# A new computed order of instructions for the first 28 slices of an attention and gated MLP kernel

## The chip, the cores and the metric

The kernel runs on one core of a Trainium2 chip. The metric is device time in microseconds (us) of one execution, taken as the median of several executions. The engines are TensorE (PE in the profile; its weight loads are PEld), VectorE (DVE), ScalarE (ACT), GpSimd (POOL) and SyncE (SP). One execution of each kernel was recorded by the hardware profiler; times inside a trace count from its first instruction. A run is called fast when it is within 1.5% of the fastest of its kernel; all comparisons below use fast runs.

## The reference, cut to what matters

```python
x: [8, 8, 512, 64]   state: [8, 8, 32, 64]
scores = x @ state^T / 8 ; a = softmax(scores)      # per batch and head
xread = a @ state                                   # 512 rows
sread = softmax(state @ x^T / 8) @ x                # 32 rows
rows = concat(xread, sread), heads side by side     # 8 * 544 rows of 512
out = (relu(rows @ w_gate) * (rows @ w_val)) @ w_out   # d_ff 1536
```

The kernel never forms xread. For each batch b it multiplies the state by the two weight matrices first (U = state @ w, in "c" and "u" units), and each of 12 slices of 128 hidden columns is then the product of U with the transposed softmax (the "gv" products). Relu on ScalarE and a multiplication on DVE turn a slice into columns of h, and "o" pieces multiply h by w_out.

## The kernel before

All parts are short functions, and a text called `program` lists the calls for the first 28 slices (all 12 of batches 0 and 1, four of batch 2). Each word is a call, and the digits behind `@` are the banks of PSUM (where this kernel's TensorE results go) that it takes. A product that takes a bank again waits for the bank's last reader: in the changed kernel's trace one began at 43.05 us, behind 0.39 us of idle time, just after that reader had ended at 42.99. A filler is a product that nobody reads; it is there only to keep TensorE busy. The instructions of an engine are issued in the order of the words, and where I compared the trace before with the words, the rows stand in that order: TensorE from 10.24 to 15.12 us. After the program a regular loop does the rest, unchanged.

```python
def u_unit(b, w, lo):                      # 512 columns of U: 8 products of 64 rows
    u_alloc(b)
    ps = held["u", b, w, lo] = [bank("up"), bank("up")]
    u_mm(ps, b, w, lo, 512)

def u_out(b, w, lo, kc, eng):              # their copy to SBUF, on act or dve
    copy[eng](out=U[b][:, w, kc, lo:lo + 512], in_=held["u", b, w, lo][kc])

def att_scale(b, jp, eng="dve"):           # word "nx": a_sn = e_sn / row sum
    ...tensor_tensor(out=by_pair(a_sn[b], jp)..., in0=e_v, in1=held["rc", b, jp]..., op=ALU.mult)

def x_next(b):                             # word "xn": casts of the next batch, then its transpose
    x_conv(b, 0, "pool")
    x_conv(b, 1, "pool")
    x_trans_dma(b)

# words: spin.n = n filler products; sc, ex, nr = scores, exponential, row sums; aT, ao = transpose
# of a_sn and its copy; re, mu = relu and multiplication of a slice; sr = state sums
for g in range(first, NF * (B + 1)):       # the loop; first = 28, so its first call is gv(2, 4)
    gv(b, jf) ... relu(b, jf) ; mult(b, jf) ; out_piece(...)
```

The softmax here doesn't subtract the row's maximum and nothing guards it: scores larger than these inputs give would overflow.

Of the kernel before, what the change touches and what calls it, by code (L numbers as in the profile page):

```python
# [16 lines left out]
def kernel(  # L17
# [52 lines left out]
    stT = const.tile([128, B, NJ, 64], BF16, name="stT")  # L70
# [5 lines left out]
    xf, xb, xT, e_sn, a_sn, ANS, U, hsb, sr_sb = {}, {}, {}, {}, {}, {}, {}, {}, {}  # L76
    copy = {"act": nc.scalar.copy, "dve": nc.vector.tensor_copy, "pool": nc.gpsimd.tensor_copy}

    given, turn = [], {"r": 0, "o": 0}

    def bank(name, kind="r"):

# [356 lines left out]
             "c": c_unit, "co": c_out, "u": u_unit, "uo": u_out, "gv": gv, "re": relu, "mu": mult, "o": out_part,  # L439
             "of": fin_x, "xn": x_next, "xp": x_pad, "sr": sr_mm, "sn": sr_norm}  # L440
    program = """
    dx.1.0.2 dx.1.1.2 stc.0.0.act stc.0.1.dve xc.0.0.act dw.0.0.128 spin.6 stT.0@5 xT.0.0@0 xc.0.1.dve dw.1.0.128 on
    sto.0.dve xT.0.1@4 xo.0.0.dve dw.0.128.128 xo.0.1.act dw.1.128.128 dw.0.256.256 spin.4 xT.0.3@2 dw.1.256.256
    xT.0.2@3 xo.0.3.dve sc.0.0@1 xo.0.2.act ex.0.0 sc.0.1@6 dw.0.512.256 xT2.1.0@5 ex.0.1 nr.0.0 xo2.1.0.act
    dw.1.512.256 spin.2 xT2.1.1@0 nr.0.1 xo2.1.1.act sc.1.0@4 dw.0.768.256 nx.0.0 dw.1.768.256 ex.1.0 spin.2
    c.1.0.128@23 nx.0.1 sc.1.1@1 co.1.0.128.1.act c.0.0.128@65 co.1.0.128.0.dve dw.0.1024.256 aT.0.1@0 ex.1.1
    co.0.0.128.0.dve aT.0.0@4 co.0.0.128.1.act ao.0.1.dve dw.1.1024.256 ao.0.0.act spin.1 c.1.128.128@32 nr.1.1
    c.0.128.128@16 co.1.128.128.1.act gv.0.0@50 co.0.128.128.0.act nr.1.0 co.0.128.128.1.act dw.0.1280.256 re.0.0
    gv.0.1@42 co.1.128.128.0.act nx.1.1 re.0.1 nx.1.0 dw.1.1280.256 c.0.256.256@17 c.1.256.256@65 co.0.256.256.1.act
    co.0.256.256.0.dve aT.1.0@3 aT.1.1@4 co.1.256.256.0.act ao.1.0.dve gv.0.2@71 dx.2.0.1 ao.1.1.dve  # L450
    co.1.256.256.1.act mu.0.1 re.0.2 gv.1.0@36 mu.0.0 ds re.1.0 mu.0.2 c.1.512.256@45 c.0.512.256@27
    co.1.512.256.0.act co.1.512.256.1.dve gv.1.1@03 co.0.512.256.1.act do.0.6 co.0.512.256.0.dve re.1.1 gv.1.4@14
    mu.1.0 xp.0 re.1.4 gv.1.3@57 mu.1.1 re.1.3 mu.1.4 gv.0.5@20 mu.1.3 do.6.12 re.0.5 gv.0.3@61 mu.0.5 xp.1 re.0.3
    c.0.768.256@35 c.0.1024.256@47 mu.0.3 co.0.768.256.1.act gv.1.2@20 co.0.1024.256.1.act co.0.768.256.0.dve df.3
    re.1.2 gv.0.4@61 co.0.1024.256.0.dve re.0.4 mu.1.2 gv.1.5@57 mu.0.4 re.1.5 gv.0.9@32 mu.1.5 re.0.9 gv.0.8@46
    mu.0.9 re.0.8 c.1.1280.256@01 c.0.1280.256@57 mu.0.8 co.1.1280.256.1.act xT2.2.1@3 co.0.1280.256.1.act
    co.1.1280.256.0.dve xT2.2.0@2 stc.1.0.pool co.0.1280.256.0.act c.1.768.256@46 xo2.2.1.dve stc.1.1.pool
    c.1.1024.256@17 xo2.2.0.act stc.3.0.pool gv.1.10@05 co.1.768.256.0.dve stc.2.0.pool co.1.768.256.1.dve
    co.1.1024.256.1.act stc.2.1.pool stT.1@3 gv.1.11@42 stc.3.1.pool re.1.10 sto.1.dve co.1.1024.256.0.act mu.1.10
    gv.0.11@76 re.1.11 re.0.11 mu.1.11 gv.1.7@30 mu.0.11 re.1.7 gv.1.9@15 mu.1.7 re.1.9 sc.2.0@4 gv.0.7@72 mu.1.9  # L460
    ex.2.0 re.0.7 nr.2.0 gv.0.6@36 re.0.6 mu.0.7 gv.0.10@01 mu.0.6 re.0.10 u.2.0.0@45 u.2.1.512@73 nx.2.0
    uo.2.0.0.1.act u.2.0.512@20 o.0.0@6 mu.0.10 uo.2.0.512.1.act uo.2.1.512.0.act uo.2.0.0.0.dve sc.2.1@5 o.0.1
    uo.2.0.512.0.act xn.3 uo.2.1.512.1.dve ex.2.1 u.2.1.1024@01 nr.2.1 u.2.1.0@42 uo.2.1.1024.0.act u.2.0.1024@35
    o.0.2 uo.2.1.0.1.act uo.2.0.1024.1.dve uo.2.1.0.0.act o.0.3@7 nx.2.1 of.0.0.dve aT.2.1@0 gv.1.8@25
    uo.2.1.1024.1.dve ao.2.1.act re.1.8 uo.2.0.1024.0.dve aT.2.0@4 o.0.4 ao.2.0.dve mu.1.8 gv.2.0@01 re.2.0 o.0.5
    mu.2.0 gv.2.2@23 of.0.1.act re.2.2 gv.1.6@45 mu.2.2 re.1.6 o.0.6@6 mu.1.6 o.0.7 o.0.8 gv.2.1@01 of.0.2.dve re.2.1
    gv.2.3@23 mu.2.1 re.2.3 o.0.9@7 mu.2.3 sr.0@4 sr.1@5 sn.0 sn.1 xp.2 xp.3
    """
    for word in program.split():
        word, _, banks = word.partition("@")  # L470
# [107 lines left out]
```

## Time and profile before

| | before |
|---|---|
| median | 224.28 us (224.14 to 224.79, 3 runs) |
| span in the trace | 222.9 us |
| first slice's product | 15.12 us |
| first product of the loop | 56.44 us |
| TensorE clock released to full speed | 10.21 us (fillers 0.427 us apart ahead of it, 0.22 after) |

The prediction below shows most of the lines. The columns are start, duration, engine, source line, operation, output and inputs, count and, in brackets, the idle time before it.

```profile
40.70 2.02 POOL L142 CAST xb<-xf 128x1024 bf16<-128x1024 f32 x2 [4.96 <-DMA xf<-in_x_dram]
```

The scaling is over before the two casts begin, at 1.0 us a cast. The 4.96 us of idle time ahead of the casts end when the transfer of x lands, so here the casts do not follow TensorE's pace.

### The profile page before, as it was taken

The numbers are of one execution on the slowest core, as the hardware profiler recorded it, in microseconds if no ns is written. First come the engines' busy times: TensorE is split into PE (matmuls) and PEld (weight loads), VectorE is DVE, ScalarE is ACT, GpSimd is POOL, SyncE is SP. The second block draws the span as 40 slices with busy tenths as digits, with TensorE's granted clock in tenths as the row PEclk, the third lists the DMA queues.
The fourth block names the chain that finished last, engine by engine and source line by source line (L and its number), as shares of the span: only waits on it lengthen the run. The fifth ranks groups of instructions, "written<-read, shape, count | busy, mean of one in ns | idle before, by whom it ended". The sixth has DMA issues, their size and how long they took to land.

```text
span 222.9 us, 4842 instructions
## 1 busy us (share of the span) xinstructions
PE 217.4 (98%) x1959; PEld 106.9 (48%) x1959; DVE 131.1 (59%) x233; ACT 123.2 (55%) x233; POOL 48.9 (22%) x54
## 2 busy tenths in 40 slices
PE   6999999999999999999999999999999999999994
PEld 2554454444544444444444444444444445666543
DVE  2399998965695559664877368646875433222100
ACT  4498788843567555574466456645654444222221
POOL 8877654300603334015000700000000000000000
PEclk9999999999999999999999999999999999999999
DMA  6999999152046771771169114511311111111132
GB/s 154 183 195 197 208 232 284 39 121 97 0 124 209 119 260 62 164 247 50 50 134 281 56 50 97 97 47 47 94 50 47 47 49 50 49 69 72 51 94 94
DMA packets 37799, 25.48 MB, mean 114 GB/s; under 512 B 18864, under 2 KB 33200, under 8 KB 37776
## 3 DMA queue, kind: packets, MB, share of 16 engines
q1 hardware_dynamic: 24912, 16.85, 26.3%
q0 software_dynamic: 11968, 7.47, 21.5%
q10 hardware_dynamic: 896, 0.85, 1.5%
q8 instruction: 15, 0.25, 0.4%
q14 instruction: 8, 0.07, 0.1%
HBM read 18.35 MB, written 8.91 MB: 122 GB/s over the span
## 4 chain that ended last, share of the span: by engine, by line
PE 95%; ACT 2%; DMA 1%; issue 0%; DVE 0%; DVEq 0%; ACTq 0%
PE o_ps L353 39%; PE gv_ps L316 38%; PE gv_ps L333 5%; PE up L291 4%; PE sc_ps L200 2%; DMA st_f<-in_state_dram 1%; PE sr_ps L264 1%; PE upc L291 1%; PE o_ps L379 1%; PE warm_ps L432 1%; PE xT_ps L186 1%; PE stT_ps L129 1%; PE xT_ps L169 1%; PE xT_ps L173 0%; ACT xT L189 0%; ACT e_sn L207 0%
## 5 line engine op out<-in xcount | busy, mean ns | idle before, releaser
L316 PE MATMUL gv_ps<-ans,U 128*128 128x512 bf16 x384 | 94.6, 379 | 0.3 <-ACT ans L249 0.3
L353 PE MATMUL o_ps<-wo_sb,h_sb 128*128 128x512 bf16 x372 | 94.8, 379 | 0.0
L340 ACT ACTIVATE g_sb<-gv_ps 128x512 bf16<-128x512 f32 (+1 forms) x108 | 62.5, 581 | 50.1 <-PE gv_ps L316 39.1
L344 DVE TENSOR_TENSOR h_sb<-gv_ps,g_sb 128x512 bf16<-128x512 f32 x96 | 64.7, 688 | 41.5 <-ACT g_sb L340 40.7
L316 PEld LDWEIGHTS <-U 128*128 128x128 bf16 x384 | 36.1, 98 | 40.7 <-issue 0.9
L353 PEld LDWEIGHTS <-h_sb 128*128 128x128 bf16 x372 | 35.3, 98 | 40.0 <-issue 1.6
L361 ACT COPY o_sb<-o_ps 128x512 f32<-128x512 f32 x29 | 17.1, 590 | 16.2 <-PE o_ps L353 16.2
L301 ACT CAST U<-up 128x512 bf16<-128x512 f32 x37 | 19.2, 594 | 11.1 <-PE up L291 11.1
L301 DVE CAST U<-up 128x512 bf16<-128x512 f32 x35 | 22.0, 682 | 2.3 <-PE up L291 1.9
L142 POOL CAST xb<-xf 128x1024 bf16<-128x1024 f32 x10 | 10.1, 1042 | 55.7 <-DMA xf<-in_x_dram 48.4
L256 POOL COPY xa<-xb 128x2048 bf16<-128x2048 bf16 (+1 forms) x9 | 15.6, 1748 | 13.9 <-issue 13.7
L213 DVE TENSOR_REDUCE cs<-e_sn 128x16 f32<-128x512 bf16 x16 | 10.9, 678 | 8.9 <-ACT e_sn L207 8.9
L344 DVE TENSOR_TENSOR hs_sb<-gv_ps,g_sb 128x256 bf16<-128x256 f32 x12 | 5.1, 425 | 15.3 <-PE gv_ps L333 10.5
L207 ACT ACTIVATE e_sn<-sc_ps 128x512 bf16<-128x512 f32 x16 | 9.7, 604 | 4.7 <-PE sc_ps L200 4.6
L219 DVE TENSOR_TENSOR a_sn<-e_sn,rc 128x512 bf16<-128x512 bf16 x16 | 11.4, 723 | 0.3
L291 PEld LDWEIGHTS <-stT 64*32 64x32 bf16 x512 | 5.9, 90 | 9.5 <-issue 8.1
L311 ACT CAST U<-upc 128x512 bf16<-128x512 f32 (+1 forms) x18 | 8.7, 542 | 0.9 <-PE upc L291 0.9
L200 PEld LDWEIGHTS <-xT 128*128 128x128 bf16 x128 | 5.9, 102 | 3.7 <-ACT xT L189 0.4
L291 PE MATMUL up<-wg_sb,stT 64*32 64x512 bf16 x144 | 7.5, 381 | 0.0
L432 PE MATMUL warm_ps<-hs_sb 128*128 128x512 bf16 x15 | 6.2, 548 | 1.2 <-DVE hs_sb L396 1.2
L333 PE MATMUL gv_ps<-br,wg_sb 128*128 128x256 bf16 x48 | 7.2, 273 | 0.0
L333 PE MATMUL gv_ps<-br,wv_sb 128*128 128x256 bf16 x48 | 7.2, 273 | 0.0
(65 smaller groups left out, 126.9 us busy)
## 6 DMA issues: line engine op xcount, KB each, us to landing
out_dram<-o_sb SPq DMA_DIRECT2D x31, 256.0 KB, 2.4
xf<-in_x_dram SPq DMA_DIRECT2D x4, 1024.0 KB, 6.1
wo_sb<-in_moe_w_out_dram POOLq DMA_DIRECT2D x2, 768.0 KB, 14.7
wg_sb<-in_moe_w_gate_dram POOLq DMA_DIRECT2D x5, 256.0 KB, 8.7
wv_sb<-in_moe_w_val_dram POOLq DMA_DIRECT2D x5, 256.0 KB, 9.3
xf<-in_x_dram POOLq DMA_DIRECT2D x1, 1024.0 KB, 15.4
xb<-in_x_dram POOLq DMA_DIRECT2D x3, 256.0 KB, 6.0
xb<-in_x_dram POOLq DMA_DIRECT2D x1, 512.0 KB, 11.7
```

The lines of the kernel that those rows point to most:

```text
L200: nc.tensor.matmul(ps[:, :, c, jj], xT[b][:, c, 2 * jp + jj], stT[:, b, 2 * jp + jj], start=True, stop=True)
L213: nc.vector.reduce_sum(out=cs, in_=e_v, axis=AX.X)
L219: {"dve": nc.vector, "pool": nc.gpsimd}[eng].tensor_tensor(out=by_pair(a_sn[b], jp).rearrange("p r (j n) -> p r j n", n=Ns), in0=e_v, in1= ...
L256: nc.gpsimd.tensor_copy(out=v[:, hs:hs + src.shape[1]], in_=src)
L291: nc.tensor.matmul(dst[parity][32 * j:32 * j + 32], stT[r:r + 64, b, j, 32 * parity:32 * parity + 32], wsb[r:r + 64, j, lo:lo + n], start= ...
L301: copy[eng](out=U[b][:, w, kc, lo:lo + 512], in_=held["u", b, w, lo][kc])
L316: nc.tensor.matmul(ps[w], U[b][:, w, kc, f0:f0 + 128], ANS[b][:, kc].rearrange("p c t -> p (c t)"), start=(kc == 0), stop=(kc == NK - 1))
L333: nc.tensor.matmul(ps[w][:, 0:nt], wsb[:, j, f0:f0 + 128], br[:, j].rearrange("p b n -> p (b n)"), start=(j == 0), stop=(j == NJ - 1))
L340: nc.scalar.activation(out=g_sb[:, 0:n], in_=ps[0][:, 0:n], func=AF.Relu)
L344: nc.vector.tensor_tensor(out=dst, in0=ps[1][:, 0:n], in1=held["g", b, jf][:, 0:n], op=ALU.mult)
L353: nc.tensor.matmul(held["o", b, tsub], src[:, jf, tsub * 128:(tsub + 1) * 128], wo_sb[:, jf], start=(jf == 0), stop=(jf == NF - 1))
L361: copy[eng](out=o_sb, in_=held["o", b, tsub])
```

## The change

The order was computed anew with recalibrated landing times and GpSimd times, and with at most two fillers in a row (after the first seven). The rows of the diff that the argument needs (the first pair only changes which of two output banks the loop takes first):

```diff
-    given, turn = [], {"r": 0, "o": 0}
+    given, turn = [], {"r": 0, "o": 1}
...
-    dx.1.0.2 dx.1.1.2 stc.0.0.act stc.0.1.dve xc.0.0.act dw.0.0.128 spin.6 stT.0@5 xT.0.0@0 xc.0.1.dve dw.1.0.128 on
-    sto.0.dve xT.0.1@4 xo.0.0.dve dw.0.128.128 xo.0.1.act dw.1.128.128 dw.0.256.256 spin.4 xT.0.3@2 dw.1.256.256
...
+    dx.1.0.2 dx.1.1.2 stc.0.0.act stc.0.1.dve dw.0.0.128 xc.0.0.dve spin.7 xT.0.0@0 xc.0.1.dve dw.1.0.128 on
+    xo.0.0.dve xT.0.1@2 dw.0.128.128 stT.0@1 xo.0.1.act dw.1.128.128 sto.0.dve spin.1 sc.0.0@3 dw.0.256.256 xT.0.2@5
+    ex.0.0 xT.0.3@4 dw.1.256.256 xo.0.2.dve xo.0.3.act nr.0.0 dw.0.512.256 spin.2 sc.0.1@6 xT2.1.0@0 ex.0.1 nx.0.0
...
+    uo.2.1.1024.0.dve uo.2.1.1024.1.act uo.2.0.1024.0.dve gv.1.10@03 uo.2.0.1024.1.act re.1.10 sc.2.0@4 o.0.1 ex.2.0
+    mu.1.10 sc.2.1@5 nr.2.0 gv.1.8@21 ex.2.1 xn.3 re.1.8 nx.2.0 o.0.2 mu.1.8 u.2.0.0@04 of.0.0.act nr.2.1 u.2.1.0@35
+    u.2.1.512@21 uo.2.0.0.0.act o.0.3@6 uo.2.1.512.1.act uo.2.0.0.1.dve uo.2.1.512.0.act o.0.4 nx.2.1 uo.2.1.0.0.act
...
+    mu.1.9 re.2.2 o.0.9@6 mu.2.2 u.2.0.512@42 sr.0@3 uo.2.0.512.1.act sr.1@5 sn.0 uo.2.0.512.0.act sn.1 xp.2 xp.3
```

More of the change, by code (lines that the diff above doesn't have):

```diff
@@ L441 @@
     program = """
-    dx.1.0.2 dx.1.1.2 stc.0.0.act stc.0.1.dve xc.0.0.act dw.0.0.128 spin.6 stT.0@5 xT.0.0@0 xc.0.1.dve dw.1.0.128 on
-    sto.0.dve xT.0.1@4 xo.0.0.dve dw.0.128.128 xo.0.1.act dw.1.128.128 dw.0.256.256 spin.4 xT.0.3@2 dw.1.256.256
-    xT.0.2@3 xo.0.3.dve sc.0.0@1 xo.0.2.act ex.0.0 sc.0.1@6 dw.0.512.256 xT2.1.0@5 ex.0.1 nr.0.0 xo2.1.0.act
-    dw.1.512.256 spin.2 xT2.1.1@0 nr.0.1 xo2.1.1.act sc.1.0@4 dw.0.768.256 nx.0.0 dw.1.768.256 ex.1.0 spin.2
-    c.1.0.128@23 nx.0.1 sc.1.1@1 co.1.0.128.1.act c.0.0.128@65 co.1.0.128.0.dve dw.0.1024.256 aT.0.1@0 ex.1.1
@@ L447 @@
-    co.0.0.128.0.dve aT.0.0@4 co.0.0.128.1.act ao.0.1.dve dw.1.1024.256 ao.0.0.act spin.1 c.1.128.128@32 nr.1.1
-    c.0.128.128@16 co.1.128.128.1.act gv.0.0@50 co.0.128.128.0.act nr.1.0 co.0.128.128.1.act dw.0.1280.256 re.0.0
-    gv.0.1@42 co.1.128.128.0.act nx.1.1 re.0.1 nx.1.0 dw.1.1280.256 c.0.256.256@17 c.1.256.256@65 co.0.256.256.1.act
-    co.0.256.256.0.dve aT.1.0@3 aT.1.1@4 co.1.256.256.0.act ao.1.0.dve gv.0.2@71 dx.2.0.1 ao.1.1.dve
-    co.1.256.256.1.act mu.0.1 re.0.2 gv.1.0@36 mu.0.0 ds re.1.0 mu.0.2 c.1.512.256@45 c.0.512.256@27
@@ L452 @@
-    co.1.512.256.0.act co.1.512.256.1.dve gv.1.1@03 co.0.512.256.1.act do.0.6 co.0.512.256.0.dve re.1.1 gv.1.4@14
-    mu.1.0 xp.0 re.1.4 gv.1.3@57 mu.1.1 re.1.3 mu.1.4 gv.0.5@20 mu.1.3 do.6.12 re.0.5 gv.0.3@61 mu.0.5 xp.1 re.0.3
-    c.0.768.256@35 c.0.1024.256@47 mu.0.3 co.0.768.256.1.act gv.1.2@20 co.0.1024.256.1.act co.0.768.256.0.dve df.3
-    re.1.2 gv.0.4@61 co.0.1024.256.0.dve re.0.4 mu.1.2 gv.1.5@57 mu.0.4 re.1.5 gv.0.9@32 mu.1.5 re.0.9 gv.0.8@46
-    mu.0.9 re.0.8 c.1.1280.256@01 c.0.1280.256@57 mu.0.8 co.1.1280.256.1.act xT2.2.1@3 co.0.1280.256.1.act
@@ L457 @@
-    co.1.1280.256.0.dve xT2.2.0@2 stc.1.0.pool co.0.1280.256.0.act c.1.768.256@46 xo2.2.1.dve stc.1.1.pool
-    c.1.1024.256@17 xo2.2.0.act stc.3.0.pool gv.1.10@05 co.1.768.256.0.dve stc.2.0.pool co.1.768.256.1.dve
-    co.1.1024.256.1.act stc.2.1.pool stT.1@3 gv.1.11@42 stc.3.1.pool re.1.10 sto.1.dve co.1.1024.256.0.act mu.1.10
-    gv.0.11@76 re.1.11 re.0.11 mu.1.11 gv.1.7@30 mu.0.11 re.1.7 gv.1.9@15 mu.1.7 re.1.9 sc.2.0@4 gv.0.7@72 mu.1.9
-    ex.2.0 re.0.7 nr.2.0 gv.0.6@36 re.0.6 mu.0.7 gv.0.10@01 mu.0.6 re.0.10 u.2.0.0@45 u.2.1.512@73 nx.2.0
@@ L462 @@
-    uo.2.0.0.1.act u.2.0.512@20 o.0.0@6 mu.0.10 uo.2.0.512.1.act uo.2.1.512.0.act uo.2.0.0.0.dve sc.2.1@5 o.0.1
-    uo.2.0.512.0.act xn.3 uo.2.1.512.1.dve ex.2.1 u.2.1.1024@01 nr.2.1 u.2.1.0@42 uo.2.1.1024.0.act u.2.0.1024@35
-    o.0.2 uo.2.1.0.1.act uo.2.0.1024.1.dve uo.2.1.0.0.act o.0.3@7 nx.2.1 of.0.0.dve aT.2.1@0 gv.1.8@25
-    uo.2.1.1024.1.dve ao.2.1.act re.1.8 uo.2.0.1024.0.dve aT.2.0@4 o.0.4 ao.2.0.dve mu.1.8 gv.2.0@01 re.2.0 o.0.5
-    mu.2.0 gv.2.2@23 of.0.1.act re.2.2 gv.1.6@45 mu.2.2 re.1.6 o.0.6@6 mu.1.6 o.0.7 o.0.8 gv.2.1@01 of.0.2.dve re.2.1
@@ L467 @@
-    gv.2.3@23 mu.2.1 re.2.3 o.0.9@7 mu.2.3 sr.0@4 sr.1@5 sn.0 sn.1 xp.2 xp.3
+    dx.1.0.2 dx.1.1.2 stc.0.0.act stc.0.1.dve dw.0.0.128 xc.0.0.dve spin.7 xT.0.0@0 xc.0.1.dve dw.1.0.128 on
+    xo.0.0.dve xT.0.1@2 dw.0.128.128 stT.0@1 xo.0.1.act dw.1.128.128 sto.0.dve spin.1 sc.0.0@3 dw.0.256.256 xT.0.2@5
+    ex.0.0 xT.0.3@4 dw.1.256.256 xo.0.2.dve xo.0.3.act nr.0.0 dw.0.512.256 spin.2 sc.0.1@6 xT2.1.0@0 ex.0.1 nx.0.0
+    xo2.1.0.act nr.0.1 dw.1.512.256 spin.2 xT2.1.1@2 xo2.1.1.act dw.0.768.256 sc.1.0@1 nx.0.1 dw.1.768.256 spin.1
@@ new lines @@
+    c.0.0.128@35 ex.1.0 aT.0.0@4 co.0.0.128.0.dve sc.1.1@6 co.0.0.128.1.act ao.0.0.dve aT.0.1@0 dw.0.1024.256 ex.1.1
+    c.1.0.128@21 nr.1.0 ao.0.1.act dw.1.1024.256 spin.1 c.0.128.128@35 c.1.128.128@46 co.1.0.128.0.act nr.1.1
+    co.0.128.128.1.act spin.2 gv.0.0@02 co.0.128.128.0.act co.1.128.128.1.act nx.1.0 dw.0.1280.256 re.0.0 gv.0.1@53
+    nx.1.1 co.1.0.128.1.act re.0.1 mu.0.0 dw.1.1280.256 c.0.256.256@67 co.1.128.128.0.act aT.1.0@0 co.0.256.256.0.act
+    co.0.256.256.1.dve c.1.256.256@15 aT.1.1@4 ao.1.0.dve co.1.256.256.1.act gv.0.2@26 dx.2.0.1 mu.0.1 ao.1.1.act
@@ new lines @@
+    co.1.256.256.0.act gv.0.3@70 re.0.2 ds gv.1.2@53 re.0.3 mu.0.2 re.1.2 mu.0.3 c.1.512.256@41 do.0.6 c.0.512.256@27
+    co.1.512.256.1.act mu.1.2 gv.1.1@65 co.0.512.256.1.act xp.0 co.1.512.256.0.dve re.1.1 gv.1.0@01 co.0.512.256.0.dve
+    re.1.0 mu.1.1 c.0.768.256@37 c.1.768.256@46 do.6.12 gv.1.5@20 mu.1.0 co.1.768.256.1.act co.1.768.256.0.dve re.1.5
+    xp.1 gv.1.4@51 co.0.768.256.0.dve re.1.4 gv.1.3@62 co.0.768.256.1.dve re.1.3 mu.1.4 df.3 gv.1.7@43 mu.1.5 re.1.7
+    gv.0.4@57 mu.1.3 re.0.4 mu.1.7 gv.0.5@61 mu.0.4 re.0.5 gv.0.7@04 mu.0.5 re.0.7 c.1.1280.256@25 c.0.1280.256@37
@@ new lines @@
+    mu.0.7 co.1.1280.256.1.act c.0.1024.256@61 xT2.2.0@0 co.0.1024.256.0.act co.0.1024.256.1.dve xT2.2.1@4
+    co.0.1280.256.0.act stc.1.0.pool co.0.1280.256.1.dve gv.0.9@56 xo2.2.0.act xo2.2.1.dve stc.1.1.pool gv.0.6@13
+    co.1.1280.256.0.dve re.0.9 re.0.6 stc.2.0.pool mu.0.9 gv.0.8@74 mu.0.6 re.0.8 stc.3.0.pool gv.0.11@05 mu.0.8
+    re.0.11 stc.2.1.pool gv.1.6@21 mu.0.11 re.1.6 stc.3.1.pool stT.1@6 gv.0.10@73 mu.1.6 sto.1.act re.0.10
+    c.1.1024.256@40 u.2.1.1024@52 mu.0.10 co.1.1024.256.1.act u.2.0.1024@61 o.0.0@7 co.1.1024.256.0.act
@@ new lines @@
+    uo.2.1.1024.0.dve uo.2.1.1024.1.act uo.2.0.1024.0.dve gv.1.10@03 uo.2.0.1024.1.act re.1.10 sc.2.0@4 o.0.1 ex.2.0
+    mu.1.10 sc.2.1@5 nr.2.0 gv.1.8@21 ex.2.1 xn.3 re.1.8 nx.2.0 o.0.2 mu.1.8 u.2.0.0@04 of.0.0.act nr.2.1 u.2.1.0@35
+    u.2.1.512@21 uo.2.0.0.0.act o.0.3@6 uo.2.1.512.1.act uo.2.0.0.1.dve uo.2.1.512.0.act o.0.4 nx.2.1 uo.2.1.0.0.act
+    aT.2.1@0 uo.2.1.0.1.act aT.2.0@1 ao.2.1.dve o.0.5 ao.2.0.act gv.2.0@42 of.0.1.act re.2.0 o.0.6@7 mu.2.0 gv.1.11@35
+    re.1.11 o.0.7 mu.1.11 gv.2.3@01 re.2.3 gv.2.1@42 mu.2.3 re.2.1 o.0.8 mu.2.1 gv.1.9@35 of.0.2.dve re.1.9 gv.2.2@01
```

## The prediction

> **What bounds the kernel now.** I read the page first (busy shares and the chain that ended last), then the table of stretches, then the chain in its first 16 us, then the rows around the place where the rewritten order hands over to the unchanged loop.
>
> ```profile
> span 222.9 us, 4842 instructions
> ...
> PE 217.4 (98%) x1959; PEld 106.9 (48%) x1959; DVE 131.1 (59%) x233; ACT 123.2 (55%) x233; POOL 48.9 (22%) x54
> ...
> PE 95%; ACT 2%; DMA 1%; issue 0%; DVE 0%; DVEq 0%; ACTq 0%
> ```
>
> TensorE holds 95% of the chain. A busy share alone would prove little, as matmul records overlap, so I took the distance from one start to the next: 0.215 to 0.216 us for 512 columns, slice after slice from 15.1 us to the end. TensorE runs back to back there. A new order of the same products can gain only where TensorE waits, or runs fillers (the spins on warm_ps), and that is before 15.1 us. The table of stretches (busy us of each engine, in brackets its instructions) says the same:
>
> ```profile
> 5.00:10.00 5.00, 4.84 (x44) 2.77 (x43) 1.55 (x4) 1.63 (x4) 4.20 (x7) 1.00 1.52 185
> 10.00:15.00 5.00, 4.82 (x131) 2.97 (x129) 4.45 (x10) 4.75 (x10) 4.35 (x6) 1.00 1.57 191
> 15.00:20.00 5.00, 4.84 (x60) 2.19 (x60) 4.93 (x12) 4.61 (x12) 2.71 (x5) 1.00 1.45 197
> 20.00:25.00 5.00, 5.00 (x61) 2.24 (x62) 4.83 (x8) 3.98 (x8) 5.00 (x5) 1.00 1.45 197
> ```
>
> After 20 us TensorE (first column) is full; before that ACT and DVE (fourth and third) are nearly full. The chain between 12 and 16 us names what holds the first slice's product:
>
> ```profile
> 12.03 1.01 ACT xT L189
> 13.04 0.50 ACT e_sn L207
> 13.54 0.26 ACT U L311
> 13.81 0.50 ACT e_sn L207
> 14.31 0.27 ACT U L311
> 14.57 0.50 ACT ans L249
> 15.07 0.04 issue
> 15.12 1.02 PE gv_ps L316 x4
> ```
>
> The first product starts at 15.12 us behind a train of ScalarE copies and exponentials, not behind a transfer.
>
> [...] here the fillers stand 0.427 us apart until the recorded clock changes at 10.21 us, and 0.22 after. [...] every row I read is in program order. [...] from a 128-row product to the 64-row U products (c and u units) the step is 0.309 us, not 0.216, and back again it costs about 0.1 to 0.19.
>
> **The change part by part.** Both orders have the same 28 slices, 10 output pieces, 12 c units, 6 u units, transposes and state products. TensorE's program grows by one load and one product: fillers go from 15 (6+4+2+2+1) to 16 (7+1+2+2+1+1+2). GpSimd issues every weight load in the same place; only two state conversions swap. So the landings stay (last w_val load 15.7 + 10.8 = 26.5 us, x of batch 2 17.5 + 11.7 = 29.2, state 30.2, w_out 34.1 and 37.7), and all but two of the waits that they could cause stay too. Evictions: ACT's list up to the last state sum goes from 69 to 73 entries, DVE's from 70 to 66, about 2 us of work; both have room after 20 us.
>
> (1) *To the first slice.* Scores of batch 0 move before two x transposes. The state copy ends near 7.2, so the first score product starts near 7.3 us instead of 8.96. That lead is lost at once: the second exponential needs the last x copy, then two ScalarE copies of 1.0 us each follow, ending near 12.9 against 13.04. From there the train is exponential 0.50, U copy 0.26, exponential 0.50, a_T copy: one U copy of 0.27 is no longer ahead, so the a_T copy may end near 14.7 instead of 15.06. But TensorE itself now has, after its last transpose (near 13.55), a c unit, a filler, two c units and two fillers; by the steps of the trace that is 13.65 + 0.34 + 0.31 + 0.34 + 2 x 0.22 = 15.08 us. First product: 15.1 against 15.12, **0.0 us**. Without the last two fillers it would be some 0.35 us earlier.
>
> (2) *Slices 2 to 27.* I walked the order bank by bank: for each unit, TensorE's place (0.865 us a slice, 0.45 a pair of c units plus switches) against the end of the eviction that frees its bank or fills its U columns (pitch 0.5 us on ACT, 0.6 on DVE, from consecutive rows). Splitting the first 256-column pair with a transpose between adds two switches, some +0.25; before had a wait of 0.2 us at 18.16 on a U copy, which goes: together **+0.05**. After that I find each eviction done 0.1 to 2 us ahead. Tightest are the slice after the 1024-column unit near 32 us and the first slice of batch 2 near 47 us, both within 0.2. The number of switches from there on is equal (1.8 us in both by the sum of my gaps). I allow **+0.05** for a miss.
>
> (3) *The hand-over.* The change moves one u unit (u.2.0.512) to the end, with only the state sums of batches 0 and 1 (sr) behind it, and both its copies stand on ACT. The loop's first slice (batch 2, columns 512 to 639) reads just these columns. Rows before the change, for the delay and for the time the state sums take:
>
> ```profile
> 39.56 0.41 PE L291 MATMUL up<-wg_sb,stT 64*32 64x512 bf16 x8
> ...
> 40.06 1.07 ACT L301 CAST U<-up 128x512 bf16<-128x512 f32 x2 [0.23 <-PE up L291]
> ```
>
> ```profile
> 55.81 0.71 PE L264 MATMUL sr_ps<-xa,e_sn 128*32 128x65 bf16 x64
> ...
> 56.45 0.82 PE L316 MATMUL gv_ps<-ans,U 128*128 128x512 bf16 x3
> ```
>
> Copies start 0.50 after the unit and two of them take 1.07, so U is there 1.57 + 0.05 = 1.62 us after it. TensorE has meanwhile the switch 0.31 and the state sums 0.64 = 0.95 us of work. It must wait 1.62 - 0.95 = **+0.67 us**. Before, these six units were copied by 46.6 us, some ten microseconds ahead of that slice.
>
> Sum: 0.0 + 0.05 + 0.05 + 0.67 = +0.77 us. In the loop nothing changes, and TensorE is the bound, so it stays to the end: 224.28 + 0.77 = 225.05, said as **225.1 us**.
>
> **The rivals.** *A: the order really gains.* Waits and fillers before 15.1 us are what it could take: fillers 15 with about half at half clock, and the ScalarE train. If the two fillers before the first slice overlap a wait I mis-timed, the first product starts at 14.8 and, with a smaller hand-over, the time is about 224.2. For it: the orders were searched on calibrated times. Against: the two 1.0 us copies stay on ScalarE in a row. *B: a new wait in the dense part.* DVE is at 4.8 to 4.9 of 5 us between 15 and 25, and one late eviction stops TensorE for 0.3 to 1 us, 225.5 to 226.1. For it: banks are reused two or three units later. Against: each step of the walk closes, and load moves from DVE to ACT, which had more room after 20 us. [...] *D: the 0.67 us is hidden.* It could be only if TensorE had other ready work; it takes instructions in order, so no.
>
> **Range and chances.** Part (3) is the firmest term (0.6 to 0.75). Part (1) is good to -0.4 to +0.3, part (2) to -0.1 to +0.7. So 8 times in 10 between 224.3 and 225.9 us. Two per cent is 4.5 us; nothing above comes near it: 1% faster, 98% same, 1% slower.
>
> **What would show it.** Right: a wait of TensorE on a ScalarE U copy, 0.6 to 0.75 us, right after the state sums and before the first product of the loop (near 57 us), and no longer wait from 20 us to there; first slice at 14.9 to 15.4 us directly behind a filler; the clock record changing between 7 and 11 us. Wrong: a first slice well before 15 us with later slices keeping the lead; a wait on a copy or a multiplication between 15 and 48 us; no wait at the hand-over[...].

Where a cut is marked above, statements were taken out. The sum: it came to +0.77 us, so 225.05, said as 225.1 us. That TensorE takes instructions in order (rival D) is shown here only by the rows from 10.24 to 15.12 us of the trace before, which stand in the order of the words.

## More of the kernel before

One more place of this trace matters later: where DVE scales a_sn of batch 2 and where GpSimd casts x of batch 3.

```profile
39.73 0.68 DVE L219 TENSOR_TENSOR a_sn<-e_sn,rc 128x512 bf16<-128x512 bf16 x1
```

## The result, and the profile after

| | before | changed |
|---|---|---|
| median of the first comparison | 224.21 us (4 runs) | 225.08 us (4 runs, 224.45 to 225.17) |
| span in the trace | 222.9 us | 223.3 us |
| clock released | 10.21 us | 4.09 us |
| first slice's product | 15.12 us | 13.85 us |
| first product of the loop | 56.44 us | 56.76 us (by its weight load; its own record is missing) |

The ratio is 1.0034, with a 95% interval of 1.0012 to 1.0056. Ratios are the mean time of one kernel's fast runs over that of the other's fast runs of the same rounds, so not quite the ratio of the medians.

The page of the changed kernel:

```profile
span 223.3 us, 4816 instructions
...
PE 213.1 (95%) x1931; PEld 105.9 (47%) x1960; DVE 130.2 (58%) x229; ACT 125.1 (56%) x237; POOL 49.4 (22%) x54
...
PE 89%; DMA 3%; DVE 2%; issue 2%; POOL 2%; ACT 1%; POOLq 0%; DVEq 0%
```

The lower busy share of TensorE is no sign of idleness: its record has 1931 products for 1960 weight loads, so 29 records are missing. The weight loads are complete, and I used them where a product's record was gone. In the chain, other engines now hold some per cent. The list of TensorE's waits between 20 and 60 us (waiting instruction, what it waited for, total us, times, longest) says where:

```profile
PE gv_ps L316 <- ACT U L301: 0.8, 1, 0.8
PE up L291 <- DVE h_sb L344: 0.4, 1, 0.4
PE o_ps L353 <- issue: 0.2, 1, 0.2
```

In the kernel before, the same list is empty between 20 us and the loop. The third line is no wait: it stands where a product's record is missing. The first wait is the predicted hand-over:

```profile
55.16 0.41 PE L291 MATMUL up<-wg_sb,stT 64*32 64x512 bf16 x8
...
55.50 0.70 PE L264 MATMUL sr_ps<-xa,e_sn 128*32 128x65 bf16 x64
55.64 1.07 ACT L301 CAST U<-up 128x512 bf16<-128x512 f32 x2 [1.07 <-PE up L291]
...
56.76 0.55 PEld L316 LDWEIGHTS <-U 128*128 128x128 bf16 x4 [0.69 <-ACT U L301]
```

The state sums take their 0.64 us to 56.14; the copies end at 56.71, and the loop's first weights load at 56.76. TensorE waited 0.62 us.

The second wait was not predicted. DVE, GpSimd and TensorE near it:

```profile
40.81 2.48 POOL L142 CAST xb<-xf 128x1024 bf16<-128x1024 f32 x2 [4.97 <-DMA xf<-in_x_dram]
40.85 1.54 DVE L219 TENSOR_TENSOR a_sn<-e_sn,rc 128x512 bf16<-128x512 bf16 x1
...
42.06 0.59 PE L291 MATMUL up<-wv_sb,stT 64*32 64x512 bf16 x9
...
42.31 0.68 DVE L344 TENSOR_TENSOR h_sb<-gv_ps,g_sb 128x512 bf16<-128x512 f32 x1
...
43.05 0.41 PE L291 MATMUL up<-wv_sb,stT 64*32 64x512 bf16 x7 [0.39 <-DVE h_sb L344]
...
43.38 1.41 PEld L353 LDWEIGHTS <-h_sb 128*128 128x128 bf16 x8 [0.23 <-issue]
```

The same step, from a U unit to the weights of the output piece behind it, in the kernel before:

```profile
42.84 0.40 PE L291 MATMUL up<-wg_sb,stT 64*32 64x512 bf16 x8
...
43.16 1.41 PEld L353 LDWEIGHTS <-h_sb 128*128 128x128 bf16 x8 [0.39 <-issue]
```

The scaling of a_sn took 1.54 us instead of 0.68, the multiplication behind it (mu.1.8) came late, and it holds the bank that a U product needs. The unit's first product (the ninth of the row at 42.06) started at 42.28 us and its second 0.76 us later, where the products of a unit otherwise start within 0.03 us of each other. From the unit's start to the next weights are 1.10 us, where 0.32 to 0.33 are usual: some 0.77 us were lost, more than at the hand-over. The casts became slower too, 2.48 us instead of 2.02.

So these two traces differ by +0.32 us at the loop in an uneven way: the changed kernel's first slice came 1.27 us earlier, and it took 1.59 us more from there to the loop.

### The profile page after: what moved, and what is told of

The parts are those of the page before. It is cut to its first block, busy times and chain, and to the rows that moved or that the text cites. A ratio compares the mean times of both kernels' runs of the same rounds, so it can differ in the third digit from the quotient of the medians.

```text
span 223.3 us, 4816 instructions
## 1 busy us (share of the span) xinstructions
PE 213.1 (95%) x1931; PEld 105.9 (47%) x1960; DVE 130.2 (58%) x229; ACT 125.1 (56%) x237; POOL 49.4 (22%) x54
## 4 chain that ended last, share of the span: by engine, by line
PE 89%; DMA 3%; DVE 2%; issue 2%; POOL 2%; ACT 1%; POOLq 0%; DVEq 0%
PE o_ps L353 38%; PE gv_ps L316 36%; PE gv_ps L333 5%; PE up L291 4%; DMA wv_sb<-in_moe_w_val_dram 3%; PE upc L291 1%; PE sc_ps L200 1%; PE o_ps L379 1%; DVE U L311 1%; PE sr_ps L264 1%; DVE h_sb L344 1%; PE aT_ps L235 1%; POOL xb L420 1%; POOL xb L412 0%; POOL wg_sb L110 0%
## 5 line engine op out<-in xcount | busy, mean ns | idle before, releaser
L316 PE MATMUL gv_ps<-ans,U 128*128 128x512 bf16 x372 | 93.6, 379 | 1.3 <-ACT U L301 0.8
L353 PE MATMUL o_ps<-wo_sb,h_sb 128*128 128x512 bf16 x358 | 92.3, 379 | 1.9 <-issue 1.7
L316 PEld LDWEIGHTS <-U 128*128 128x128 bf16 x384 | 36.1, 98 | 41.1 <-ACT U L301 0.7
L301 ACT CAST U<-up 128x512 bf16<-128x512 f32 x39 | 20.4, 595 | 12.2 <-PE up L291 12.2
L361 ACT COPY o_sb<-o_ps 128x512 f32<-128x512 f32 x30 | 17.7, 590 | 16.4 <-PE o_ps L353 16.4
L142 POOL CAST xb<-xf 128x1024 bf16<-128x1024 f32 x10 | 10.6, 1088 | 56.3 <-DMA xf<-in_x_dram 56.3
L301 DVE CAST U<-up 128x512 bf16<-128x512 f32 x33 | 20.8, 683 | 2.3 <-PE up L291 1.9
L256 POOL COPY xa<-xb 128x2048 bf16<-128x2048 bf16 (+1 forms) x9 | 15.6, 1750 | 13.1 <-issue 12.8
L219 DVE TENSOR_TENSOR a_sn<-e_sn,rc 128x512 bf16<-128x512 bf16 x16 | 12.1, 762 | 0.4
L291 PE MATMUL up<-wv_sb,stT 64*32 64x512 bf16 x144 | 7.4, 379 | 0.4 <-DVE h_sb L344 0.4
```

The costliest lines, as they stand in the source:

```text
L219: {"dve": nc.vector, "pool": nc.gpsimd}[eng].tensor_tensor(out=by_pair(a_sn[b], jp).rearrange("p r (j n) -> p r j n", n=Ns), in0=e_v, in1= ...
L256: nc.gpsimd.tensor_copy(out=v[:, hs:hs + src.shape[1]], in_=src)
L291: nc.tensor.matmul(dst[parity][32 * j:32 * j + 32], stT[r:r + 64, b, j, 32 * parity:32 * parity + 32], wsb[r:r + 64, j, lo:lo + n], start= ...
L316: nc.tensor.matmul(ps[w], U[b][:, w, kc, f0:f0 + 128], ANS[b][:, kc].rearrange("p c t -> p (c t)"), start=(kc == 0), stop=(kc == NK - 1))
L353: nc.tensor.matmul(held["o", b, tsub], src[:, jf, tsub * 128:(tsub + 1) * 128], wo_sb[:, jf], start=(jf == 0), stop=(jf == NF - 1))
L361: copy[eng](out=o_sb, in_=held["o", b, tsub])
```

## The experiments

Theory at the outset: the change loses 0.6 us at the hand-over and 0.57 us near 43 us by the meeting of the scaling with the cast, and its start is worth nothing. (The 0.57 us was a wrong reading; the trace has 0.77, as shown above. The expectations still carry it.) Rivals: the waits are only shifted ones, or the new start gains and later parts eat it. The runs came on two chips, on which the kernel before had medians of 224.16 us (12 runs) and 225.07 us (11 runs); each run is compared with its own. One kernel's executions scatter by more than 1 us. The diffs are cut to the words that move; line breaks and renamed banks are left out.

**a_uearly: the last U unit ahead of the last slice.**

```diff
- re.1.9 gv.2.2@01 mu.1.9 re.2.2 o.0.9@6 mu.2.2 u.2.0.512@42 sr.0@3 uo.2.0.512.1.act sr.1@5 sn.0 uo.2.0.512.0.act sn.1
+ re.1.9 u.2.0.512@42 gv.2.2@01 uo.2.0.512.1.act mu.1.9 re.2.2 uo.2.0.512.0.act o.0.9@6 mu.2.2 sr.0@3 sr.1@5 sn.0 sn.1
```

> The changed kernel with the last U unit (batch 2, gate columns 512 to 1023) and its two copies moved ahead of the last slice, still on ScalarE. Theory (hand-over wait, 0.64 us in the changed kernel's trace): the wait before the loop's first product vanishes and the time falls from 225.1 to about 224.45 us. Rival (that wait only takes the place of another one, or the loop has slack that takes it up): the time stays at 225.0 to 225.2.

Five fast runs had a median of 224.0 us, ratio 0.9999 (0.9978 to 1.0019). The profiled run is not usable: it took 788.1 us, with a mean of 1.10 us for one product of a slice (L316), where the trace before has 0.38. Its page has no row of clock, and its mean granted clock is given as 1.0.

**uearly_again: the same kernel.**

> The changed kernel with the last U unit ahead of the last slice, again, since the profiled run of the first try took 786 us and shows nothing. Theory: no wait before the loop's first product, 0.6 us below the changed kernel of the same rounds. Rival: no difference.

Measured 224.61 us, ratio 1.0016 (0.9988 to 1.0044). The trace at the hand-over:

```profile
55.81 0.71 PE L264 MATMUL sr_ps<-xa,e_sn 128*32 128x65 bf16 x64
56.67 0.81 PE L316 MATMUL gv_ps<-ans,U 128*128 128x512 bf16 x3 [0.16 <-issue]
```

The first product's record is missing again; its weight load is at 56.44 us, right at the end of the state sums (55.81 + 0.64). The wait is gone. The 11 fast runs of both tries have a median of 224.47 us, against 225.16 us of the changed kernel on the same chip: 0.69 us for a wait of 0.62 us. The theory of the hand-over holds, and the loop has no slack behind it.

**b_ulate: the reverse, in the kernel before.**

```diff
- u.2.0.0@45 u.2.1.512@73 nx.2.0 uo.2.0.0.1.act u.2.0.512@20 o.0.0@6 mu.0.10 uo.2.0.512.1.act ... uo.2.0.512.0.act ...
- o.0.9@7 mu.2.3 sr.0@4 sr.1@5 sn.0 sn.1
+ u.2.0.0@45 u.2.1.512@73 nx.2.0 uo.2.0.0.1.act o.0.0@6 mu.0.10 ...
+ o.0.9@7 mu.2.3 u.2.0.512@45 sr.0@2 uo.2.0.512.1.act sr.1@3 sn.0 uo.2.0.512.0.act sn.1
```

> The kernel before with that same U unit moved to the end, behind the last output piece, both copies on ScalarE, nothing else. Theory: a wait of about 0.65 us before the loop's first product and 224.2 + 0.65 = about 224.85 us. Rival (a late unit costs nothing by itself): 224.2.

Measured 225.31 us against 224.16, ratio 1.0044 (1.0024 to 1.0064), so some 1.0 us, more than expected. Its trace:

```profile
55.00 0.71 PE L264 MATMUL sr_ps<-xa,e_sn 128*32 128x65 bf16 x64
55.14 1.07 ACT L301 CAST U<-up 128x512 bf16<-128x512 f32 x2 [1.07 <-PE up L291]
...
56.50 0.81 PE L316 MATMUL gv_ps<-ans,U 128*128 128x512 bf16 x3 [0.79 <-DVE sn L273]
```

The profile blames the last DVE step, but again the first product's record is missing: its weights load at 56.27 us, just after the copies end at 56.21. From the end of the state sums (55.64) that is a wait of 0.63 us. The mechanism is shown in both directions; the remaining 0.4 us of the median lie within the interval.

**a_mufirst: the multiplication ahead of the slow scaling.**

```diff
- ex.2.1 xn.3 re.1.8 nx.2.0 o.0.2 mu.1.8
+ ex.2.1 xn.3 re.1.8 mu.1.8 o.0.2 nx.2.0
```

> The changed kernel with one DVE multiplication (slice 8 of batch 1) ahead of the scaling of a_sn of batch 2 instead of behind it. Theory: in the changed kernel the scaling took 1.54 us instead of 0.68 beside a GpSimd cast and held the multiplication back, so that a U product waited some 0.57 us for its bank near 43 us; now that wait goes and the time is about 224.5 us, with the scaling still slow (over 1.2 us) beside the cast. Rival (the wait comes from ScalarE or from the loading of the bank): wait and time stay, 225.1.

Measured 225.22 us, ratio 1.0044 (1.0018 to 1.0069): no gain. The trace shows the wait near 43 us gone and another one come, and the loop's first weights load at 57.14 us, later than in the changed kernel:

```profile
42.15 1.25 DVE L219 TENSOR_TENSOR a_sn<-e_sn,rc 128x512 bf16<-128x512 bf16 x1
```

```profile
PE aT_ps L235 <- DVE a_sn L219: 0.8, 1, 0.8
```

The scaling, still slow beside a cast, now delays the row sums and the second scaling, and the transposes of a_sn wait at 45.5 us. So my expectation fell: moving one victim of the meeting hands the delay to the next one.

**a_both: both edits.**

> Both moves together. Theory (two separate waits on the path, no slack behind either): gains add, 1.2 us, about 223.9 us, 0.3 us below the kernel before. Rival (one hides the other): 224.4 to 224.5.

Measured 225.0 us, ratio 1.0042 (1.0022 to 1.0062), neither the theory's 223.9 nor the rival's 224.4. One of the six runs has a mean granted clock of 0.992 (see below), and the profiled one (224.38 us) shows no wait at the hand-over. With a_mufirst worthless, only the hand-over's gain was left, and the median does not show even that. This run stays unexplained.

**a_scfirst: the first scores of batch 2 one slice earlier, so the scaling comes before the cast.**

```diff
- gv.1.10@03 uo.2.0.1024.1.act re.1.10 sc.2.0@4 o.0.1 ex.2.0 mu.1.10 sc.2.1@5 nr.2.0 gv.1.8@21 ex.2.1 xn.3 re.1.8 nx.2.0 o.0.2 mu.1.8
+ sc.2.0@4 ex.2.0 gv.1.10@03 uo.2.0.1024.1.act nr.2.0 re.1.10 o.0.1 nx.2.0 mu.1.10 sc.2.1@5 gv.1.8@21 ex.2.1 xn.3 re.1.8 o.0.2 mu.1.8
```

> The changed kernel with the first scores of batch 2 one slice earlier, so that the scaling of a_sn of batch 2 runs before GpSimd's cast of batch 3 begins (near 40.8 us) and not beside it. Theory ([...]): the scaling takes 0.68 us again, no wait of a U product near 43 us nor of a transpose near 45 us, 225.1 - 0.57 = about 224.5 us. Rival (DVE is simply behind there): the scaling is quick but a wait of 0.4 to 0.7 us stays between 42 and 46 us, 225.1.

(The clause cut here put the theory as a rule; behind it stood the changed kernel's trace, with 1.54 us for the scaling that met the casts and 0.68 for the one after them, at 44.33 us.)

In its trace scaling and casts do not meet, both have their normal lengths, and there is no wait between 20 us and the hand-over:

```profile
39.86 0.69 DVE L219 TENSOR_TENSOR a_sn<-e_sn,rc 128x512 bf16<-128x512 bf16 x1
```

```profile
40.55 2.02 POOL L142 CAST xb<-xf 128x1024 bf16<-128x1024 f32 x2 [5.06 <-DMA xf<-in_x_dram]
```

The loop's first product comes at 55.95 us, 0.81 us earlier than in the changed kernel. Of this, 0.26 is an earlier first slice (13.59 us), and 0.77 is the wait that went, less 0.22 for a longer wait on a weight transfer near 15.5 us (0.38 against 0.16 us). The profiled run took 224.28 us. The median is 225.56 us against 225.07, ratio 1.0033 (1.0008 to 1.0058), which is no gain; two of the six runs had a mean granted clock of 0.990. The trace bears the mechanism out; a gain in the median is not shown.

**a_scfirst_u: the same with the early U unit.**

> The same, and the last U unit ahead of the last slice as in the earlier run. Theory: both losses go, 225.1 - 0.57 - 0.64 = about 223.9 us, a little below the kernel before (224.2). Rival (something else has the rest of the loss): 224.3 or more.

Measured 224.93 us against 225.07, ratio 1.0013 (0.9977 to 1.0049): equal to the kernel before, not clearly below it. The profiled run (227.27 us) was the slowest of the six. Its clock was released at 4.42, taken back at 7.84 for 6.83 us (the granted share is 0.50 between 8 and 12 us) and released again at 14.66; the first slice started at 17.17 us. In this late run the scaling fell into the second cast after all, and took 1.47 us: the repair depends on the start. The return of the clock was new to me and led to a_lowfill.

**h1_newstart: the changed order up to the first two slices, then the old one** (banks renamed so that each suffix finds its banks free).

```diff
- spin.6 stT.0@5 xT.0.0@0 ... gv.0.1@42 co.1.128.128.0.act nx.1.1 re.0.1 nx.1.0 dw.1.1280.256 | c.0.256.256@17 ...   (before)
+ spin.7 xT.0.0@0 ... gv.0.1@53 nx.1.1 co.1.0.128.1.act re.0.1 mu.0.0 dw.1.1280.256 co.1.128.128.0.act | c.0.256.256@17 ...
```

> The kernel before with the changed kernel's order up to its first two slices, and its own order after that (banks renamed to fit). Theory (as predicted, the new start is worth nothing at the same clock): 224.2 us, within 0.3. Rival (the new start really leads, and the later losses ate more than 0.9 us): 223.6 or less.

Measured 224.99 us against 225.07, ratio 1.0001 (0.9978 to 1.0024): the start is worth nothing in time.

**h2_oldstart: the old start, then the changed order.**

```diff
- ... gv.0.1@53 nx.1.1 co.1.0.128.1.act re.0.1 mu.0.0 dw.1.1280.256 | c.0.256.256@67 ...   (changed)
+ ... gv.0.1@42 co.1.128.128.0.act nx.1.1 re.0.1 nx.1.0 dw.1.1280.256 mu.0.0 | c.0.256.256@67 ...
```

> The changed kernel with the order of the kernel before up to the first two slices. Theory (all of the loss lies after the start): as the changed kernel, 225.1 us within 0.3, with the wait at the hand-over 0.6 to 0.7 us and the one near 43 us. Rival (the new start leads by 0.5 us): 225.6 or more.

Measured 225.89 us against 225.07, ratio 1.0035 (1.0001 to 1.0068), the same ratio as the changed kernel's 1.0034. The loss lies after the start. Its trace happens to show the other side of the meeting:

```profile
40.63 0.69 DVE L219 TENSOR_TENSOR a_sn<-e_sn,rc 128x512 bf16<-128x512 bf16 x1
```

```profile
40.74 2.46 POOL L142 CAST xb<-xf 128x1024 bf16<-128x1024 f32 x2 [5.45 <-DMA xf<-in_x_dram]
```

Here DVE began 0.11 us before GpSimd and was not slowed; the casts were, by 0.44 us. Near 43 us nothing waited. The hand-over cost its 0.63 us.

**after_again: the changed kernel, unaltered.**

> The changed kernel once more, unaltered, for a second trace and six more times beside the others. Theory: slower than the kernel before by 0.3 to 0.4%, a wait of 0.6 to 0.7 us at the hand-over in the trace whatever the start does; the wait near 43 us only if the scaling of batch 2 begins inside GpSimd's cast. Where the start is late, the clock record shows a return to half clock before 15 us.

Measured 225.16 us against 224.16, ratio 1.0045 (1.0025 to 1.0064). The scaling started at 40.94 us inside the first cast and took 1.45 us; the losses are 0.69 us near 43 us (0.68 between two starts of one unit) and 0.62 us at the hand-over. Its first slice came at 13.54 us, 0.31 earlier than in the first trace, and its loop at 56.77, no earlier: a longer wait for a weight transfer near 16 us took the lead away. One of six runs had a mean clock of 0.990.

**a_lowfill: the changed kernel without five fillers.**

```diff
- sto.0.dve spin.1 sc.0.0@3 ... dw.0.512.256 spin.2 sc.0.1@6 ... dw.1.512.256 spin.2 xT2.1.1@2
+ sto.0.dve sc.0.0@3 ... dw.0.512.256 sc.0.1@6 ... dw.1.512.256 xT2.1.1@2
```

> The changed kernel without the five fillers between the first x transposes and the last ones (7 at the start and the last 4 stay). Theory (with short runs of fillers the clock is granted early and then taken back in some runs; fewer fillers make that common): a mean granted clock below 0.993 in at least half of the runs, where the changed kernel has it in few, and a median 1 to 3 us above the changed kernel. Rival (the fillers only stand in waits and the clock does not care): the time stays within 0.4 us of the changed kernel and the mean clock at 0.998 or more.

Measured 226.33 us, ratio 1.0088 (1.0069 to 1.0107), and four of six runs had a mean granted clock of 0.985 (226.2 to 226.7 us). The theory holds: with these fillers gone the low mean clock comes in four of six runs, with them in 8 of 51 (below). Not all of the loss is the clock, though: the two runs without that took 225.8 us, and the profiled one of them waited 0.8 us for a weight transfer near 16.5 us. What a return to half clock looks like is seen in the table of stretches of h1_newstart (first column after the stretch is its length; PE's busy time, PEclk is the third value from the end). First the changed kernel, whose clock stayed, then h1_newstart, whose clock was taken back from 7.62 to 11.03 us:

```profile
4.00:8.00 4.00, 2.63 (x39) 1.65 (x39) 1.76 (x5) 1.23 (x3) 4.00 (x7) 1.00 1.27 151
8.00:12.00 4.00, 3.65 (x74) 2.24 (x74) 3.39 (x8) 3.38 (x5) 2.85 (x5) 1.00 1.69 180
```

```profile
4.00:8.00 4.00, 1.97 (x22) 1.06 (x21) 2.17 (x5) 1.69 (x3) 3.69 (x6) 0.95 1.32 189
8.00:12.00 4.00, 4.00 (x52) 2.67 (x54) 2.80 (x6) 1.83 (x3) 2.56 (x4) 0.62 1.67 179
```

TensorE was at work for less than half of the stretch ahead of the return. Cut at the recorded clock changes instead, the 3.41 us from the release on (so long the clock stayed in the two traces that lost it) hold 1.76 us of TensorE's work in h1_newstart and 1.63 in a_scfirst_u, those two, and 2.04 (the changed kernel) to 2.99 us in the ten early traces that kept it. Where between lies the limit, and whether busy time is the measure, these runs do not tell. Over all runs but a_lowfill, 8 of 51 fast runs with the new start have a mean clock of 0.992 or less, and none of the 41 with the old start (23 of the kernel before beside the experiments, 6 each of b_ulate, h2_oldstart and h2_u_act).

**h2_u_act: a candidate.** Old start, changed order, early U unit, and the cast of batch 3 on ScalarE.

```diff
- ... ex.2.1 xn.3 re.1.8 nx.2.0 ... ao.2.0.act ...
+ ... ex.2.1 re.1.8 nx.2.0 ... ao.2.0.act xn.3.act ...
```

> Candidate: the old start, the changed order after it, the last U unit ahead of the last slice, and the cast of batch 3 on ScalarE near 46 us instead of GpSimd near 41 us. Theory (hand-over and the meeting of scaling and cast are the losses of the changed order, the old start keeps its clock): every scaling before 60 us takes 0.68 us, no wait from 20 us to the loop, 0.2 to 0.5 us below the kernel before. Rival: as the kernel before, within 0.2 us.

In its trace both scalings near 42 us take 0.69 us or less and TensorE waits nowhere for a copy or a scaling from 20 us to the loop, whose first product comes at 55.84 us. The median is 224.53 us against 224.16, ratio 1.0006 (0.999 to 1.0022): as the kernel before, not better. In the traces the loop runs at one pace (a_lowfill alone loses 0.4 us in it), and yet this candidate takes 166.9 us from its first product to the end of the span where the kernel before takes 166.5: its last product keeps its lead of 0.61 us, and the rest goes after it. No version clearly beat the kernel before.

## Why the prediction was right or wrong

The number was right, 225.1 predicted and 225.08 measured, and so was "no change at 2%". The hand-over was right by its mechanism too; the agreement of the rest is partly luck. Several of the prediction's own signs came out against it: a wait between 15 and 48 us that it listed as a sign of being wrong, longer (0.77 us) than the one at the hand-over; the clock record changing at 4.09 us and not between 7 and 11; and the first slice at 13.85 us and not at 14.9 to 15.4, though directly behind a filler as it said. By its steps:

- **Hand-over, +0.67 us: right.** Measured 0.62 to 0.64 us in the traces that have the late unit, 0.69 us in medians when it is taken away, and put into the kernel before it appears there.
- **First slice, 0.0 us: right as a difference, wrong as times.** h1_newstart has a ratio of 1.0001. But 15.1 us for either kernel came from a trace with a clock released at 10.21 us. With the clock released at 4.1 to 6.6 us, the first slice comes at 13.3 to 14.0 us with the old start (three traces) and 13.5 to 14.3 us with the new one (six traces, a_lowfill left out). I took one run's clock for the kernel's.
- **Slices 2 to 27, +0.05 and +0.05 us: wrong in its making, nearly right in its sum.** The walk gave the scaling of a_sn its usual length and did not ask what GpSimd does beside it; in the changed kernel the wait that follows is 0.77 us (0.69 in the second trace), and 0.16 us are lost at 15.9 us, where the other early traces name a weight transfer. On the other side stand waits in the old order that I did not count, since the trace before, with its late first slice, has neither: in b_ulate, which has the old order there, 0.37 us on the weight transfer near 15.6 us and 0.49 us on GpSimd's state conversion at 32.0 us (the profile shows 0.34 of it, and a wait on a copy at 30.9 us that is only a missing record). From first slice to loop, the changed kernel's trace against b_ulate's without its hand-over wait comes to 42.91 against 42.33 us, so +0.58 us, of which the hand-over is 0.62. My sum for the rest was +0.10, the traces have -0.04: 0.93 us of waits in one order and 0.86 in the other nearly cancel, which no step of the walk foresaw. That was luck.
- **Rival B** (a late eviction, 0.3 to 1 us) did occur in the traces, made by GpSimd and not by DVE's load. Its cost in the median is not settled: taking it away changed the traces, but no median clearly.
- **Rival C** (a later release of the clock): its size and the stretch it looked at rested on no trace. What the runs show is a return: 8 of 51 runs of the new start have a mean clock of 0.992 or less, and the traces of two of them show the clock taken back. That the shorter rows of fillers are the reason is what a_lowfill supports, by taking more of them away (four of six runs). I had looked for a later release, not for a return. A sum of rival B was off as well: 225.05 + 0.3 is 225.4 and not 225.5.

What the traces show of the meeting: each scaling that began inside a cast ended 0.53 to 0.55 us after that cast's end, whatever its own start (42.39 after 41.85, 43.40 after 42.87, and in the loop of both kernels 84.24 after 83.70), and in h2_oldstart the scaling that began first kept its 0.69 us while the casts took 2.46 us, not 2.02. The scaling reads both its inputs from SBUF. The multiplication of a slice has one input in PSUM and kept its 0.69 us beside casts (at 41.54 us in a_mufirst, at 70.40 in the trace before). That the place of the inputs makes the difference was not shown: no run varied it alone.

## What to carry to other kernels

When one engine is full and an order is rewritten, look first at the seam to the code that follows: a unit put last must still be copied before the next reader, and only the work between the two can hide that (with nothing but the 0.64 us of state sums between them, TensorE waited 0.62 us here). Check a DVE operation like the scaling here (0.68 us apart from the casts, up to 1.54 when it began inside one) against GpSimd work whose start is set by a transfer, and keep the two apart rather than reordering their victims. Fillers that seem useless in one trace may be what keeps the clock in others (a low mean clock in four of six runs without five of them, in 8 of 51 with them), so read several traces of a start before shortening them. And measure a wait from start to start against the same step elsewhere: the profile's idle time near 43 us is 0.39 us where 0.77 were lost, and in b_ulate a missing record makes a wait at 30.9 us that was none.
